# A written order for the opening of a chunked-attention and mixture kernel: 128-token loads, own PSUM banks, later units moved

## The chip, the cores and the metric

The kernel runs on one NeuronCore of a Trainium2 chip. The metric is the device time of one execution in microseconds (us). TensorE is PE here, its weight loads PEld, VectorE DVE, ScalarE ACT, GpSimd POOL and SyncE SP; SP issues nearly all DMA transfers.

## The reference

Queries, keys and values are 8 x 8 x 576 x 64 in float32. Attention goes over chunks of 64 tokens that don't see each other; its output is one row of 512 numbers for each of 4608 tokens, which then goes through a root-mean-square norm and a gated layer of width 1536.

```python
scores = scale * np.matmul(q_c, k_c.transpose(0, 1, 2, 4, 3))     # chunks of 64
scores = scores - np.max(scores, axis=-1, keepdims=True)
attn = np.exp(scores)
attn = attn / (np.sum(attn, axis=-1, keepdims=True) + 1e-09)
out = np.matmul(attn, v_c)
...
rms = np.sqrt(np.mean(x * x, axis=-1, keepdims=True) + 1e-06)
xn = x / rms * rms_g
g = xn @ w_gate
silu = g * (1.0 / (1.0 + np.exp(-g)))
val = xn @ w_val
return (silu * val @ w_out).astype(np.float32)
```

## The kernel before

**Numbers in two parts.** The large products keep float32 accuracy by splitting each number into a high part and a low part, which PE multiplies fast (hi·hi, lo·hi, hi·lo: three products for one). The activations are split when x is turned: ACT writes the high part xh with the norm's weight (`x_split`, L523), DVE the low part xl (L524). The weights arrive as float32 in `raw` tiles of 1 MB and are converted once, in 18 conversions: on ACT an absolute value and a scaling (L189, L190), on DVE a clamp, a shift and two word operations (L198, L199, L200, L203; the last is a custom instruction on 16-bit words), on ACT a cast to the high part (L214), on DVE the subtraction that leaves the low part (L220). `conv_start`, `conv_join` and `conv_end` are these three pieces; `conv_step` does one step of each for three neighbouring conversions and starts the next load.

**Tiles and units.** The tokens form nine tiles of 512. Attention goes by units of 256 tokens, two to a tile; a unit has two blocks of 128 tokens. For a block: scores on PE (`scores`, L269), maximum and subtraction on DVE (L282, L283), exponential on ACT (L286), sums and their reciprocal on DVE (L291 to L293), transposing of the weights through PE (L329) with a copy on ACT (L330), values on PE (L451), division by the sums on DVE (L482), mean square on ACT (L470), an addition on DVE (L471), a power on POOL (L473), scaling on ACT (L488), transposing of x on PE (L554), and the split.

**Tile 0.** Units 0 and 1 are the opening; the scheduler of the framework decides in which order each engine takes the opening's instructions. Then come twelve steps f of the gated layer: `gated` does the up products of 128 columns (L565), the gate on ACT (L583) and DVE (L587), and `down` the products with the output weights (L629). During these steps the weights are converted, ahead of the step that multiplies by them, and units 2 and 3 are computed for tile 1 (scores at f 0 and 5, transposes at f 2 and 7, values at f 3 and 8, scaling at f 4 and 9).

**Tiles 1 and 2, and the pairs.** From tile 1 on the order on PE, DVE, ACT, SP and POOL is that of the code. Tiles 1 and 2 have 24 half-steps each (up products in L606, gate in L619 and L621). The remaining six tiles go in pairs with seven products in place of eight (L794, L975), whose combined weights ("sides", L659 to L676, L695 to L729) are made in tiles 1 and 2. Units 4 to 9 are computed there, at the half-steps that a table `UNIT_AT` gives, a row for a unit. Their weights are turned by way of memory: `turn_away` (L367) and `turn_back` (L377, into tile eT), values in L392, x turned by DVE (L423), sent away (L428) and brought back (L435). All of these transfers stand in SP's one queue.

## Time and profile before

| | |
|---|---|
| three runs | 903.3, 905.18, 905.21 us; median 905.18 |
| the profiled execution | 903.54 us, its span 901.8 us |
| PE busy in the span | 875.2 us, 97% |
| PEld, DVE, ACT, POOL busy | 79%, 75%, 49%, 19% |
| granted PE clock, mean | 0.998 of full |

The span is the time between the first and the last recorded instruction; 1.7 us of the execution lie outside of it. A share of the whole span is a mean over the opening, tile 0, tiles 1 and 2 and the pairs, which load the engines differently.

### The profile page before, as it was taken

The numbers are of one execution on the slowest core, as the hardware profiler recorded it, in microseconds if no ns is written. First come the engines' busy times: TensorE is split into PE (matmuls) and PEld (weight loads), VectorE is DVE, ScalarE is ACT, GpSimd is POOL, SyncE is SP. The second block draws the span as 40 slices with busy tenths as digits, with TensorE's granted clock in tenths as the row PEclk, the third lists the DMA queues.
The fourth block names the chain that finished last, engine by engine and source line by source line (L and its number), as shares of the span: only waits on it lengthen the run. The fifth ranks groups of instructions, "written<-read, shape, count | busy, mean of one in ns | idle before, by whom it ended". The sixth has DMA issues, their size and how long they took to land.

```text
span 901.8 us, 17138 instructions
## 1 busy us (share of the span) xinstructions
PE 875.2 (97%) x6792; PEld 715.4 (79%) x6792; DVE 672.1 (75%) x1083; ACT 438.1 (49%) x733; POOL 171.6 (19%) x213
## 2 busy tenths in 40 slices
PE   5799999999999999999999999999999999999998
PEld 4588878877888888888877888888878888888886
DVE  6999996788686887876577988756679974345885
ACT  5997944446353663433355644334536532112452
POOL 0100005395670000112221001122210002111000
PEclk9999999999999999999999999999999999999999
DMA  9698966879879967489877884898689677445623
GB/s 358 267 376 311 312 242 218 268 240 289 252 232 312 293 240 266 162 308 350 259 271 233 302 300 164 303 291 316 238 255 330 256 297 266 152 156 191 217 72 116
DMA packets 96512, 231.82 MB, mean 257 GB/s; under 512 B 7344, under 2 KB 63664, under 8 KB 81072
## 3 DMA queue, kind: packets, MB, share of 16 engines
q1 hardware_dynamic: 95376, 230.19, 73.9%
q8 instruction: 54, 0.88, 0.4%
q10 hardware_dynamic: 1056, 0.52, 0.2%
q14 instruction: 26, 0.21, 0.1%
HBM read 171.97 MB, written 58.72 MB: 256 GB/s over the span
## 4 chain that ended last, share of the span: by engine, by line
PE 74%; DVE 8%; issue 6%; ACT 6%; DMA 4%; POOL 1%; SPq 1%; ACTq 0%; DVEq 0%; POOLq 0%
PE ps_a L794 10%; PE ps_c L794 10%; PE ps_b L794 10%; PE ps_a L975 7%; PE ps_b L975 7%; PE ps_c L975 6%; PE ps_d L794 5%; PE ps_g L606 5%; PE ps_v L606 4%; PE ps_d L975 4%; PE ps_s L269 1%; PE ps_o L392 1%; DMA wr<-wsd 1%; PE acc L629 1%; DVE ab L723 1%
## 5 line engine op out<-in xcount | busy, mean ns | idle before, releaser
L894 ACT CAST gh<-g 128x512 fp32r<-128x512 f32 x140 | 81.7, 620 | 75.5 <-PE ps_b L975 21.3
L895 DVE TENSOR_TENSOR gl<-g,gh 128x512 fp32r<-128x512 f32 x140 | 95.3, 688 | 30.3 <-ACT gh L894 29.3
L794 PE MATMUL ps_c<-xp,wr 128*128 128x512 f32 x432 | 104.7, 391 | 0.0
L794 PE MATMUL ps_b<-xp,wr 128*128 128x512 f32 x432 | 104.4, 391 | 0.0
L794 PE MATMUL ps_a<-xp,wr 128*128 128x512 f32 x432 | 103.7, 390 | 0.4 <-DMA wr<-wsd 0.4
L794 PEld LDWEIGHTS ps_a<-xp,wr 128*128 128x128 f32 x432 | 80.9, 188 | 17.6 <-issue 0.8
L794 PEld LDWEIGHTS ps_c<-xp,wr 128*128 128x128 f32 x432 | 80.7, 188 | 17.1
L794 PEld LDWEIGHTS ps_b<-xp,wr 128*128 128x128 f32 x432 | 80.6, 188 | 16.9
L859 POOL TENSOR_TENSOR g<-c,c 128x512 f32<-128x512 f32 x18 | 23.2, 1291 | 359.1 <-DVE c L855 269.0
L606 PE MATMUL ps_g<-xh,parts 128*128 128x512 f32 x192 | 65.8, 396 | 1.1 <-ACT sg L619 1.1
L606 PE MATMUL ps_v<-xh,parts 128*128 128x512 f32 x192 | 66.2, 398 | 0.0
L975 PE MATMUL ps_a<-gh,wo 128*128 128x512 f32 x176 | 55.9, 389 | 0.0
L794 PE MATMUL ps_d<-xp,wr 128*128 128x512 f32 x216 | 51.9, 389 | 0.0
L975 PE MATMUL ps_c<-gh,wo 128*128 128x512 f32 x160 | 51.1, 392 | 0.2 <-ACT gh L894 0.2
L975 PE MATMUL ps_b<-gh,wo 128*128 128x512 f32 x160 | 50.5, 389 | 0.0
L794 PEld LDWEIGHTS ps_d<-xp,wr 128*128 128x128 f32 x216 | 40.5, 188 | 8.4
L937 DVE TENSOR_TENSOR g<-g 128x512 f32<-128x512 f32 x68 | 46.6, 686 | 0.0
L835 ACT ACTIVATE c<-c 128x512 f32<-128x512 f32 x18 | 11.4, 635 | 68.1 <-DVE c L855 68.0
L606 PEld LDWEIGHTS ps_v<-xh,parts 128*128 128x128 f32 x192 | 36.3, 189 | 10.1 <-issue 2.1
L606 PEld LDWEIGHTS ps_g<-xh,parts 128*128 128x128 f32 x192 | 36.5, 190 | 9.6 <-ACT sg L619 1.6
L844 DVE TENSOR_TENSOR u<-ps_b,p 128x512 f32<-128x512 f32 x36 | 24.0, 685 | 25.2 <-PE ps_b L794 24.0
L695 POOL TENSOR_TENSOR ab<-parts 128x256 f32<-128x256 f32 x48 | 37.3, 810 | 23.5 <-DVE xl L524 23.5
(176 smaller groups left out, 1872.3 us busy)
## 6 DMA issues: line engine op xcount, KB each, us to landing
wr<-wsd SPq DMA_DIRECT2D x63, 1024.0 KB, 8.5
qk<-qk_dram SPq DMA_DIRECT2D x17, 1024.0 KB, 6.9
wo<-wol SPq DMA_DIRECT2D x16, 1024.0 KB, 8.0
raw<-w_up_dram SPq DMA_DIRECT2D x12, 1024.0 KB, 13.0
wo<-wod SPq DMA_DIRECT2D x12, 1024.0 KB, 9.4
vt<-v_dram SPq DMA_DIRECT2D x18, 512.0 KB, 5.8
wsd<-parts SPq DMA_DIRECT2D x18, 512.0 KB, 8.3
wo<-wol SPq DMA_DIRECT2D x16, 512.0 KB, 7.6
```

What stands on the lines that cost most here:

```text
L269: nc.tensor.matmul(st["s"][j][c * CH : (c + 1) * CH, pr], st["q"][rows, pr, tok : tok + CH], st["k"][rows, pr, tok : tok + CH], start=True ...
L392: nc.tensor.matmul(st["o"][(2 * c + t) * Q : (2 * c + t + 1) * Q, h * D : (h + 1) * D], eT[rows, c, t, h], vt[rows, c, h], start=True, sto ...
L606: nc.tensor.matmul(ps[k], a, b[dt], start=(dt == 0 and i == 0), stop=(dt == NDT - 1 and i == 2), skip_group_check=True,)
L695: return nc.gpsimd.tensor_tensor(out, one, two, op=op)
L794: nc.tensor.matmul(ps, w[:, a, m, cols], xp[:, b, kt], start=start and kt == 0 and i == 0, stop=stop and kt == 1 and i == 2, skip_group_ch ...
L835: nc.scalar.activation(t, t if src is None else src, AF.Silu)
L844: nc.vector.tensor_tensor(kp["u2"], b["b"], kp["p1"], op=add)
L859: nc.gpsimd.tensor_tensor(g[1][1], kp["c22"], kept[0]["c22"], op=mult)
L894: nc.scalar.copy(gh, src)
L895: nc.vector.tensor_tensor(gl, src, gh.bitcast(F32), op=ALU.subtract)
L937: nc.vector.tensor_tensor(out, one, two, op=ALU.subtract)
L975: nc.tensor.matmul(ps[m][INTO[p]], w[:, m, a], parts[c], start=p in FROM and i == 0 and j == 0, stop=p in LAST and i == NPR - 1 and j == 2 ...
```

## The change

- Queries and keys are laid out by blocks of 128 tokens, so that a block's are 4 KB in one piece for each partition. The opening loads four blocks by four transfers of 512 KB on SP, ahead of the values, the weights and the norm's weight; four more weight tiles follow the first where three did.
- The whole opening, from the loads to the last split, is put under a written order for five engines. `softmax`, `norm`, `x_transpose_unit`, `conv_start` and `conv_join` are cut into pieces for it. Maximum and subtraction alternate for the two halves of a block. The scores of each block have own PSUM banks. The transposed weights go to the tiles `gl` and `gh`. The reciprocals of two blocks are taken at once.
- The mean square uses the function of the later units (`mean_square`): addition and power both on POOL.
- Only conversion 0 is done in the opening. The ACT part of conversions 2 to 7 is tied behind the last high part of the split (`tokens_first`).
- The first up products take all of hi·xh of gate and value first, then lo·xh, then hi·xl (`up_first`).
- Unit 2 is computed at f 1, 3, 4 and 5, unit 3 at f 6, 8, 9 and 10.
- In `UNIT_AT`, units 6 and 7 load their values, take back the turned weights and multiply by the values at earlier half-steps (unit 6: 16, 16, 25 become 13, 15, 18; unit 7: 27, 27, 32 become 20, 21, 26), and what follows moves with them.

```diff
+LATER = 7
+UNITS_AT = {1: (2, 0), 3: (2, 1), 4: (2, 2), 5: (2, 3), 6: (3, 0), 8: (3, 1), 9: (3, 2), 10: (3, 3)}
...
-    (5, 10, 16, 12, 14, 16, 25, 27, 27, 28, 31),
-    (11, 15, 27, 17, 19, 27, 32, 34, 34, 35, 38),
+    (5, 10, 13, 12, 14, 15, 18, 20, 20, 21, 25),
+    (11, 15, 20, 17, 19, 21, 26, 28, 28, 29, 32),
...
+    def tokens_first(ins, n):
+        if 1 < n <= LATER:
+            info = mybir.DependencyInfo(mybir.DependencyClass.NoSync, mybir.DependencyReason.DATA)
+            tc.add_manual_dep(ins.ins, first_last[0].ins.name, info, reason="tokens are split first")
...
-    def load_first_unit():
-        qt, kt = (x[:, 2 * i : 2 * i + 2].rearrange("p s (a t) -> p (s a) t", t=UT) for i in range(2))
-        for s in range(2):
-            part = slice(s * P, (s + 1) * P)
-            nc.sync.dma_start(qt[:, :, part], qk[0][:, 0, :, part])
-            nc.scalar.dma_start(kt[:, :, part], qk[0][:, 1, :, part])
-            state[s] = {"q": qt, "k": kt}
+    def load_sub(i, t):
+        t = t.rearrange("p (w a t) -> p w a t", w=2, t=P)
+        nc.sync.dma_start(t, qk[i // 2][:, i % 2])
+        state[i] = {"q": t[:, 0], "k": t[:, 1]}
...
+    def up_first():
+        pg, pv = bank(ps_h, "ps_g"), bank(ps_h, "ps_v")
+        for i in range(3):
+            for ps, wh, wl in ((pg, wgh, wgl), (pv, wvh, wvl)):
+                a, b = ((wh, xh), (wl, xh), (wh, xl))[i]
+                for dt in range(NDT):
...
-    load_first_unit()
+    first_ordered = tc.manual_schedule(engines={*engines, mybir.EngineType.Pool})
+    first_ordered.__enter__()
+    for i in range(2):
+        load_sub(i, x[:, 2 * i : 2 * i + 2].rearrange("p s c -> p (s c)"))
...
     conv_load(0)
-    load_values(0)
-    load_unit(1)
+    nc.sync.dma_start(g_col, rms_g)
     load_values(1)
...
+    norm_square(3)
+    conv_words(0)
+    x_split_half(0, 0)
+    norm_scale(2)
+    x_split_half(0, 1)
+    conv_high(0)
+    norm_scale(3)
+    for half in range(2):
+        x_transpose_half(1, half, ps_acc)
+    conv_end(0)
+    for half in range(2):
+        x_split_half(1, half)
+    conv_start(1)
+    first_ordered.__exit__(None, None, None)
+    conv_step(EARLY - 1)
```

DVE in the later part of the opening, before, with the weight conversions among the attention's instructions (L198 and L199 clamp and shift, L200 and L203 word operations, L220 a low part of weights, L524 low parts of x):

```order
41 L199 TENSOR_SCALAR w<-w 128x1024
42 L524 SCALAR_TENSOR_TENSOR xl_125<-ps_x,g_col,xh_121 128x256
43 L471 TENSOR_SCALAR ss<-ss 128x1
44 L200 SCALAR_TENSOR_TENSOR w<-raw,w 128x1024
45 L220 TENSOR_TENSOR parts<-w,parts 128x1024
46 L524 SCALAR_TENSOR_TENSOR xl_126<-ps_x,g_col,xh_122 128x256
49 L203 ISA w<-raw,w 128x2048
51 L198 TENSOR_SCALAR w<-w 128x1024 x2
52 L199 TENSOR_SCALAR w<-w 128x1024 x2
53 L200 SCALAR_TENSOR_TENSOR w<-raw,w 128x1024
54 L524 SCALAR_TENSOR_TENSOR xl_123<-ps_x,g_col,xh_119 128x256
56 L203 ISA w<-raw,w 128x2048
```

The same place after the change (L220 and L223 are now the word operations, L249 the low part of weights, L569 the low part of x, L212 and L213 clamp and shift):

```order
33 L220 SCALAR_TENSOR_TENSOR w<-raw,w 128x1024
34 L223 ISA w<-raw,w 128x2048
35 L569 SCALAR_TENSOR_TENSOR xl_123<-ps_x,g_col,xh_119 128x256
36 L569 SCALAR_TENSOR_TENSOR xl_124<-ps_x,g_col,xh_120 128x256
39 L249 TENSOR_TENSOR parts<-w,parts 128x1024
42 L569 SCALAR_TENSOR_TENSOR xl_125<-ps_x,g_col,xh_121 128x256
43 L569 SCALAR_TENSOR_TENSOR xl_126<-ps_x,g_col,xh_122 128x256
44 L212 TENSOR_SCALAR w<-w 128x1024
45 L213 TENSOR_SCALAR w<-w 128x1024
46 L220 SCALAR_TENSOR_TENSOR w<-raw,w 128x1024
47 L212 TENSOR_SCALAR w<-w 128x1024
48 L223 ISA w<-raw,w 128x2048
```

Clamps, shifts and word operations of conversions 1 to 3 stood ahead of the last xl; they stand behind it now, and only the word operations of conversion 0 are ahead of the first.

ACT at the splits after the change, with what each instruction waits for in brackets (L568 high parts of x, L533 scaling of a block, L237 cast of a conversion's high part, L190 and L194 the ACT part of conversions):

```order
17 L568 ACTIVATE xh_119<-ps_x,g_col 128x256 [waits DMAHW6_49,PE_49]
18 L568 ACTIVATE xh_120<-ps_x,g_col 128x256 [waits DVE_49]
19 L533 ACTIVATE x<-x,ri_t 128x512 [waits Activation_49,Pool_49]
20 L568 ACTIVATE xh_121<-ps_x,g_col 128x256 [waits PE_49]
21 L568 ACTIVATE xh_122<-ps_x,g_col 128x256 [waits DVE_49]
22 L237 CAST parts<-w 128x1024
23 L533 ACTIVATE x<-x,ri_t 128x512 [waits Activation_49,Pool_49]
24 L568 ACTIVATE xh_119<-ps_x,g_col 128x256 [waits PE_49]
25 L568 ACTIVATE xh_120<-ps_x,g_col 128x256 [waits DVE_49]
28 L190 ACTIVATE w<-raw 128x1024 [waits DMAHW0_49]
29 L194 ACTIVATE raw<-raw 128x1024
```

Every second high part waits for DVE (the low part that reads the same bank), and L190 and L194 of conversions from 1 on stand behind all high parts; before, four of L189 and six of L190 stood ahead of the last one, one of each for conversion 0.

SP in tile 1, before, at unit 6 (L367 and L377 send away and bring back the turned weights of unit 6, L428 sends x of unit 5, L676 stores combined weights, L245 loads the values of unit 6):

```order
87 L367 DMA away_e12_2203<-e_1984 128x512
88 L367 DMA away_e13_2205<-e_1991 128x512
89 L428 DMA away_x5_2220<-xu_2118 128x1024
90 L676 DMA wol_130<-parts_926 512x1x256 x2
91 L245 DMA vt_2304<-v_dram 128x1024
92 L377 DMA eT_2306<-away_e12_2203 32x4x256 x2
93 L377 DMA eT_2306<-away_e13_2205 32x4x256 x2
94 L728 DMA wsd_128<-side_2270 128x512
```

And after the change (L413, L423, L474, L742 in their places; the values are loaded at row 84):

```order
84 L275 DMA vt_2170<-v_dram 128x1024
89 L413 DMA away_e12_2205<-e_1984 128x512
90 L413 DMA away_e13_2207<-e_1991 128x512
91 L474 DMA away_x5_2222<-xu_2118 128x1024
92 L423 DMA eT_2224<-away_e12_2205 32x4x256 x2
93 L423 DMA eT_2224<-away_e13_2207 32x4x256 x2
94 L742 DMA wol_130<-parts_924 512x1x256 x2
```

The four loads of eT stand one place behind unit 5's x now, with the values ahead of them and the stores behind.

## Rows read from the trace of the kernel before

**Rows 1.** The page, part 1: busy us of each engine, its share of the span, and its instructions.

```profile
PE 875.2 (97%) x6792; PEld 715.4 (79%) x6792; DVE 672.1 (75%) x1083; ACT 438.1 (49%) x733; POOL 171.6 (19%) x213
```

**Rows 2.** Busy time by stretch, the opening and tile 0: start and end (us), length, busy us of each engine with its instructions, granted PE clock as a share of full, DMA share, GB/s.

```profile
0.00:37.24 37.24, 21.18 (x294) 15.65 (x294) 27.66 (x62) 25.89 (x41) 4.44 (x11) 1.00 0.90 353
37.24:132.00 94.76, 93.19 (x651) 76.50 (x651) 92.69 (x121) 78.09 (x149) 2.75 (x2) 1.00 0.83 296
```

**Rows 3.** Timeline of PE: start (us), duration, line, operation, out<-in, count, and in brackets the idle time before it with what ended it.

```profile
4.88 1.13 PE L269 MATMUL ps_s<-x 64*64 64x64 f32 x32 [4.88 <-DMA x<-qk_dram]
6.63 1.13 PE L269 MATMUL ps_s<-x 64*64 64x64 f32 x32 [0.62 <-DMA x<-qk_dram]
...
33.10 1.11 PE L554 MATMUL ps_x<-ident,x 128*128 128x128 f32 x4 [3.53 <-ACT x L488]
34.42 0.80 PE L565 MATMUL ps_g<-xh,parts 128*128 128x512 f32 x1 [0.20 <-ACT xh L523]
...
37.24 0.65 PE L565 MATMUL ps_g<-xh,parts 128*128 128x512 f32 x1
...
123.83 0.50 PE L565 MATMUL ps_g<-xh,parts 128*128 128x512 f32 x1 [1.57 <-ACT sg L583]
...
190.37 0.39 PE L606 MATMUL ps_v<-xl,parts 128*128 128x512 f32 x1 [1.92 <-issue]
...
208.74 0.39 PE L606 MATMUL ps_v<-xh,parts 128*128 128x512 f32 x1
...
212.76 0.50 PE L606 MATMUL ps_g<-xh,parts 128*128 128x512 f32 x1 [1.14 <-ACT sg L619]
```

**Rows 4.** Transfers from 0 to 60 us, in 40 slices of 1.5 us: GB/s moved in each.

```profile
GB/s 0 122 338 326 421 388 426 423 424 405 404 410 431 431 421 415 415 399 437 431 404 401 399 90 5 0 0 5 344 268 289 399 431 363 254 362 447 431 421 379
```

**Rows 5.** Groups of DVE's instructions from 20.8 to 38.2 us: line, operation, out<-in with shapes, count | busy us, mean ns of one | idle time before.

```profile
L524 DVE SCALAR_TENSOR_TENSOR xl<-ps_x,g_col,xh 128x256 fp32r<-128x256 f32 x8 | 3.7, 480 | 0.7 <-ACT xh L523 0.7
...
L200 DVE SCALAR_TENSOR_TENSOR w<-raw,w 128x1024 int32<-128x1024 int32 x2 | 2.4, 1219 | 0.0
L203 DVE CUSTOM_DVE_ANT_0 w<-raw,w 128x2048 uint16<-128x2048 uint16 x2 | 2.4, 1218 | 0.0
L198 DVE TENSOR_SCALAR w<-w 128x1024 f32<-128x1024 f32 x3 | 2.0, 689 | 0.0
L199 DVE TENSOR_SCALAR w<-w 128x1024 int32<-128x1024 int32 x3 | 1.9, 674 | 0.0
L482 DVE TENSOR_TENSOR x<-ps_o,rs 128x256 f32<-128x256 f32 x4 | 1.6, 418 | 0.7 <-PE ps_o L451 0.7
L291 DVE TENSOR_REDUCE rs<-e 128x8 f32<-128x512 f32 x1 | 0.7, 686 | 0.0
L293 DVE RECIPROCAL rs<-rs 128x8 f32<-128x8 f32 x2 | 0.4, 196 | 0.0
L292 DVE TENSOR_SCALAR rs<-rs 128x8 f32<-128x8 f32 x2 | 0.3, 164 | 0.0
```

**Rows 6.** Timeline of ACT in the opening and at the first gate.

```profile
21.20 0.47 ACT L523 ACTIVATE xh<-ps_x,g_col 128x256 fp32r<-128x256 f32 x1
...
26.13 1.05 ACT L214 CAST parts<-w 128x1024 fp32r<-128x1024 f32 x1
...
27.47 0.72 ACT L488 ACTIVATE x<-x,ri 128x512 f32<-128x512 f32 x1
...
38.39 1.15 ACT L190 ACTIVATE raw<-raw 128x1024 int32<-128x1024 uint32 x1
39.55 1.28 ACT L583 ACT_TABLE_LOAD   x1
40.85 0.60 ACT L583 ACTIVATE sg<-ps_g 128x512 f32<-128x512 f32 x1
```

**Rows 7.** Timeline of POOL in the opening.

```profile
25.98 1.46 POOL L473 TENSOR_TENSOR ri<-ss,mhalf 128x1 f32<-128x1 f32 x1 [6.94 <-DVE ss L471]
```

**Rows 8.** Timeline of DVE: the last low parts of x, the last low part of weights in tile 0, and tile 1 at the turning of x and the softmax of unit 6.

```profile
37.22 0.88 DVE L524 SCALAR_TENSOR_TENSOR xl<-ps_x,g_col,xh 128x256 fp32r<-128x256 f32 x2 [0.71 <-ACT xh L523]
...
129.61 1.22 DVE L220 TENSOR_TENSOR parts<-w,parts 128x1024 fp32r<-128x1024 f32 x1
130.74 0.42 DVE L667 TENSOR_TENSOR w<-w 128x256 f32<-128x256 f32 x1
...
204.11 1.25 DVE L423 STREAM_TRANSPOSE xu<-xu 128x1024 f32<-128x1024 f32 x1 [0.46 <-ACT xu L417]
...
205.85 0.41 DVE L341 TENSOR_REDUCE mx<-ps_s 128x4 f32<-128x256 f32 x1
206.30 0.42 DVE L342 TENSOR_TENSOR e<-ps_s,mx 128x256 f32<-128x256 f32 x1
```

**Rows 9.** Tile eT from 200 to 260 us: duration min/median/max in ns with first and last start, and the times from issue to landing.

```profile
L392 PE MATMUL ps_o<-vt,eT x256: 213/216/240, 230.0 to 253.3; 64*32 64x64 f32 x128
...
DMA to landing us min/median/max: 4.3/4.9/5.6
```

**Rows 10.** Timeline of SP in tile 1: transfers issued.

```profile
205.38 0.32 SPq L428 DMA_DIRECT2D away_x<-xu  x1
...
208.60 2.74 SPq L377 DMA_DIRECT2D eT<-away_e  x4
```

**Rows 11.** Busy time by stretch after the gap before 190.37 (columns as in rows 2).

```profile
191.19:194.61 3.42, 3.42 (x10) 2.63 (x9) 3.28 (x9) 1.55 (x4) 3.01 (x7) 0.50 0.91 243
```

More of the change, by code (lines that the diff above doesn't have):

```diff
@@ L181, in conv_load, with conv_abs, conv_low @@
             nc.sync.dma_start(raws[n], w_up[f] if kind == "up" else w_out[f // 2])
+    def conv_abs(n):
+        words = raws[n].bitcast(I32).rearrange("p (n w) -> p n w", w=2)
+        low, high = words[:, :, 0], words[:, :, 1]
+        w = wp.tile([P, 2 * DM], F32, name="w")
+        conv[n] = low, high, w
+        tokens_first(nc.scalar.activation(w, high.bitcast(F32), AF.Abs, scale=2.0**16), n)
+    def conv_low(n):
+        low = conv[n][0]
+        tokens_first(nc.scalar.mul(low, low.bitcast(U32), 2.0**-29), n)
@@ L188, in conv_start, with conv_clamp, conv_words @@
-            conv[n] = low, high, w
-            nc.scalar.activation(w, high.bitcast(F32), AF.Abs, scale=2.0**16)
-            nc.scalar.mul(low, low.bitcast(U32), 2.0**-29)
+            conv_abs(n)
+            conv_low(n)
+    def conv_clamp(n):
+        w = conv[n][2]
+        wi = w.bitcast(I32)
+        nc.vector.tensor_scalar(w, w, HIGH_LEAST, HIGH_MOST, op0=ALU.max, op1=ALU.min)
+        nc.vector.tensor_single_scalar(wi, wi, 3, op=ALU.logical_shift_left)
+    def conv_words(n):
+        low, high, w = conv[n]
+        wi = w.bitcast(I32)
+        nc.vector.scalar_tensor_tensor(
+            wi, high, -(2**31), wi, op0=ALU.bitwise_and, op1=ALU.bitwise_or
+        )
+        nc.vector.tensor_tensor(wi, wi, low, op=ALU.add)
@@ new lines, in conv_high @@
+    def conv_high(n):
+        w = conv[n][2]
+        parts = wts.tile([P, 2, 2, DM], F32R, tag="wts", name="parts")
+        (conv_parts if pairs[n][0] == "up" else out_parts).append(parts)
+        conv[n] = w, parts
+        kind, f = pairs[n]
+        if kind == "up":
+            homes = (wgh, wgl, f), (wvh, wvl, f)
+        else:
+            homes = (woh, wol, f), (woh, wol, f + 1)
+        for i, (hi, lo, at) in enumerate(homes):
+            hi[at], lo[at] = parts[:, 0, i], parts[:, 1, i]
+        nc.scalar.copy(parts[:, 0].rearrange("p i c -> p (i c)"), w)
@@ L205, in conv_join @@
-            (conv_parts if pairs[n][0] == "up" else out_parts).append(parts)
-            conv[n] = w, parts
-            kind, f = pairs[n]
-            if kind == "up":
-                homes = (wgh, wgl, f), (wvh, wvl, f)
-            else:
-                homes = (woh, wol, f), (woh, wol, f + 1)
-            for i, (hi, lo, at) in enumerate(homes):
-                hi[at], lo[at] = parts[:, 0, i], parts[:, 1, i]
-            nc.scalar.copy(parts[:, 0].rearrange("p i c -> p (i c)"), w)
+            conv_clamp(n)
@@ L216, in conv_end @@
+            conv_words(n)
+            conv_high(n)
     def conv_end(n):
-        if 0 <= n < len(pairs):
+        if n in conv:
             w, parts = conv.pop(n)
@@ L1080, in __call__ @@
             self.n += 1
-    load_first_unit()
+    engines = mybir.EngineType.PE, mybir.EngineType.SP, mybir.EngineType.DVE, mybir.EngineType.Activation
+    first_ordered = tc.manual_schedule(engines={*engines, mybir.EngineType.Pool})
+    first_ordered.__enter__()
+    for i in range(2):
+        load_sub(i, x[:, 2 * i : 2 * i + 2].rearrange("p s c -> p (s c)"))
+    t = io.tile([P, 2, 2, NPAIR, P], F32, tag="qk", bufs=1, name="qk")
+    for s in range(2):
+        load_sub(2 + s, t[:, s].rearrange("p w a t -> p (w a t)"))
@@ L1096, in tile_chunk_attn_swiglu @@
-    softmax_sum(0)
-    att_transpose(1)
+    for i in range(2):
+        softmax_less(i)
+        softmax_exp(i)
+    copied = att_transpose(0, later=True)
+    scores(2, s2)
+    softmax_sum(0)
+    copied()
+    copied = att_transpose(1, later=True)
+    scores(3, s3)
+    softmax_sum(1)
+    softmax_turned(0)
+    copied()
+    softmax_less(2)
+    softmax_exp(2)
+    conv_abs(0)
     o = two_banks(ps_h, "ps_o")
     att_values(0, o)
-    softmax_sum(1)
+    copied = att_transpose(2, later=True)
@@ L1115, in tile_chunk_attn_swiglu @@
+    att_values(3, o)
+    norm_scale(0)
     norm(2)
-    att_values(3, o)
+    norm_square(2)
+    norm_scale(1)
+    for half in range(2):
+        x_transpose_half(0, half, ps_a)
     norm(3)
-    x_transpose_unit(1)
-    conv_start(0)
-    conv_step(EARLY)
+    norm_square(3)
[8 more added lines that the diff above has]
+    conv_end(0)
+    for half in range(2):
+        x_split_half(1, half)
@@ L1161, in tile_chunk_attn_swiglu @@
         evacuate(acc, 0, s)
-    engines = mybir.EngineType.PE, mybir.EngineType.SP, mybir.EngineType.DVE, mybir.EngineType.Activation
     ordered = tc.manual_schedule(engines=set(engines))
@@ L1311 @@
     arrays = {
[L1312 removed]
+        "qk": np.stack([heads_first(q), heads_first(k)], axis=3),
         "v": vv,
```

160 lines of the change are left out of this document (87 added, 73 removed).

## The prediction

> **What bounds the kernel now.** I read the engines' shares first: PE is busy 875.2 of 901.8 us, no other engine over three quarters [rows 1]. Then the span is cut where the matmuls become continuous. Up to 37.24 us PE has only 21.18 us of work, which is the opening that the change writes down anew; from 37.24 to 132 it is busy 93.19 of 94.76 [rows 2]. The reader should see the other column of that second row: DVE is busy 92.69 of the same 94.76. In tile 0, where the weights are converted, DVE is as full as PE, with 2.07 us to spare; ACT has 16.67.
>
> PE's timeline shows where it stands still, with the wait in brackets: the first score waits 4.88 for queries and keys, the last transposes 3.53 for the scaled x, the first product of the MoE comes at 34.42; from 37.24 the products are continuous, with gaps of 1.57, 1.92 and 1.14 before 123.83, 190.37 and 212.76 [rows 3]. So time can be won in the opening, and it stays won only if DVE, next in line, lets PE keep its lead.
>
> **The loads.** The first block's scores wait for its queries and keys until 4.88, the second's until 6.63 [rows 3]. They come in pieces of 512 bytes. In the transfer row the slices of 1.5 us from 3 to 6 us moved 338 and 326 GB/s, and those from 6 us on about 420 [rows 4]. After, pieces are 4 KB and these 512 KB come alone. At 420 GB/s they take 1.25 us; from the slice that begins at 1.5 us (122 GB/s, transfers starting in it) that gives 3.6 at the earliest. I bound the landing by 3.6 and by 4.88, and take 4.4.
>
> The row gives the 512-byte pieces a fifth less. The Trainium skill, "DMA: Bandwidth & Descriptors", section Specifications, puts the least size for line rate at 512 bytes; by that the new layout would gain nothing and the landing stay at 4.88, half a microsecond in the sum.
>
> **DVE through the opening.** After, DVE's order is a straight line from the first scores to the first splits. From 4.4 the scores take 1.13 [rows 3], so DVE starts at 5.5. Four blocks of reduce and subtract: the new order makes them dependent pairs, j by j, and such a pair stands later in the trace at 205.85 and 206.30 [rows 8]: 0.45 from start to start, and 0.34 for the second, since neighbours overlap by about 0.08 (129.61 + 1.22 ends 0.09 after 130.74). So 2 x 0.79 = 1.58 a block, 6.3 in all; the old order, two of each kind in a row, has no such pairs. The other pieces by their means, less 0.08 each: four sums at 0.60 make 2.4, two turnings at 0.08 + 0.12 0.4, eight norm halves at 0.34 2.7, the clamp and shift of conversion 0 at 0.60 1.2, its two word operations at 1.14 2.3 [rows 5]. A sum that needs the exponential just before it, and a turning that needs its sums, can't overlap; I add 0.08 for each of some ten of these, 0.8. In all 16.1: DVE reaches the first low split at 21.6 if it never waits. Between 6.01 (4.88 + 1.13) and 37.24 it idled 31.23 - 27.66 = 3.6 [rows 2, 3]; I take half of that, 1.8, and get 23.4 (21.6 to 25.2).
>
> Then ACT and DVE alternate, since the second high part of a bank waits for DVE's low part of the first: low 0.48, high 0.47, the scale of block 2 0.72, high 0.47, low 0.48, high 0.47, the cast of conversion 0 1.05, the scale of block 3 0.72, its transposes 1.11 of which half before the first bank is full, high 0.47 [rows 3, 5, 6]. That is 5.9, less the overlap of 0.08 where two stand in a row on ACT 5.7: the first MoE product at about 29.1 instead of 34.42, 5.3 earlier (bounds 27.2 to 30.9). Four further splits, alternating at about 0.95 each but the first, end at 31.9 instead of 37.22 + 0.88 = 38.10 [rows 8]: 6.2 earlier.
>
> **Moves that cost nothing by themselves.** The mean square's addition leaves DVE (0.15 a block) for POOL, where the power of one column took up to 1.46 [rows 5, 7]; an addition of one column is bounded by nothing and by that, and I take 1 between them. It lies beside DVE's norms for blocks 0 to 2; block 3's has the 2.3 of words and three splits as cover, and without that cover it costs 1. Own banks for the scores and the gl and gh homes of the transposed weights let PE run ahead of DVE; PE isn't what is waited for there. The product order of the first up needs the high parts only, for 8 products. Units 2 and 3 keep their instructions; unit 3 is scaled at f 10 in place of 9 and its x is turned at f 11, so a step of 94.76 / 12 = 7.9 us covers it; the uncovered price would be its two scalings, 1.4 [rows 2, 6].
>
> **What is owed.** Here I expect the gain to go. By 38.10 the old DVE order had finished, besides conversion 0, the clamps and shifts of conversions 1 to 3 and the word operations of 1 and 2: from 20.8 to 38.2 three clamps (L198, 0.69), three shifts (L199, 0.67) and two of each word operation (L200, L203, 1.22) [rows 5]. Less 0.08 each that is 1.8 + 1.8 + 2.3 + 2.3 = 8.1 us of DVE work that the change puts behind the last split. The last split is 6.2 earlier, so DVE is 1.9 later in tile 0 than now, less the 2.07 of idle that it can use [rows 2]: -0.2 to +1.9. The conversions are what PE multiplies by, and the last low part, from 129.61, is ready 1.2 us before tile 0's end at 132 [rows 8]; so PE can end the tile between 1.4 earlier and 1.9 later. Not all idle can be used, as DVE waits for ACT's casts, which start late too: I take +0.6. The 5.3 us won up front show up as waits for converted weights, spread over tile 0.
>
> ACT gets four more table loads in tile 0: 1.28 each [rows 6], 5.1 of its 16.67 idle; hidden, except where a cast stands behind one. The row shows the next instruction starting 0.02 after the load ended (39.55 + 1.28, then 40.85), and the one before it ended as it began: no drain is seen.
>
> The Trainium skill, "ScalarE: Activation LUTs", section What ACT_TABLE_LOAD costs, gives a switch 1.283 us for the load and 1.38 for a drain, 2.66 in all. By it the four take 10.6 us of ACT, an estimate from that page, and the sum would rise by up to 5.5.
>
> **Tile 1.** Unit 6's values move from half-step 25 to 18. Now they start at 230.0, and their transposed weights, issued from 208.60 on and 4.3 to 5.6 us in landing, are there some 14 us ahead [rows 9, 10]. After, they are issued right behind unit 5's x, which leaves at 205.38 when DVE's turn of 204.11 + 1.25 is done [rows 8, 10]; SP holds them behind that. From 205.7 the first lands at 210.0 or later, a fourth issued about 1.5 behind and landing in 4.9 at 212.1 [rows 9]. PE reaches half-step 18 at 208.74 [rows 3]. It waits 1.3 to 3.4, with the down and up products queued behind. Most of now's 1.14 before 212.76 goes into that wait, as ACT catches up: net +0.2 to +2.3. I take +0.3, near the landing's minimum, as 1 MB of stores now goes behind these pieces. The gap of 1.92 before 190.37 has no releaser in the trace; I keep it.
>
> **Sum.** 903.54 + 0.6 + 0.3 = 904.4 against the profiled run's own time. The three runs of before have a mean of 904.56, 1.02 above that run; with that 905.5, which I give as the median.
>
> **Rivals.**
> - *The lead is kept.* If the new interleaving packs DVE and ACT better than I assume, 5.3 comes off: 898.2, with the 1.02 899.3; half of it gives 901.9. For it: PE idles 16 of the first 37 us. Against: DVE's 92.69 of 94.76. Decided by whether DVE's last conversion ends before 127. Chance 0.30.
> - *Slower by the late transfer.* Place: PE at half-step 18. A wait of 3.4, less the 1.14, is +2.3; and after the 1.92 gap the clock was granted at 0.50 from 191.19 to 194.61, the lower level of 1.2 GHz [rows 11], where the 3.42 cost 1.7. Together +4.0, with 0.6 for tile 0: 909.2. It decides once the last piece lands after 211. Against: after the 1.57 before 123.83 the clock stayed [rows 2]. Chance 0.14.
> - *The opening is not shorter.* POOL at 1.46 an operation and the word operations ahead of the splits eat half the 6.2: then DVE is 8.1 - 3.1 - 2.07 = 2.9 late, 907.8. Chance 0.07.
> - *The table loads aren't hidden.* If each of the four stands in front of a cast that PE waits for, 4 x 1.28 = 5.1 come on top: 910.6. Against: 16.67 of idle on ACT, and the 0.02 above. Chance 0.05. (The rule of that page of the Trainium skill would act in this way.)
>
> **How the numbers follow.** The forecast has 0.44. A measurement of this kernel tells about 0.2%, 1.8 us, from no change, since its three runs differ by that: 903.4 to 907.0 is "same". Faster is the first rival, 0.30; slower the three others, 0.26. The forecast's own range, by the bounds of tile 0 and tile 1, is 903 to 908. To hold 8 in 10 the range takes in the greater part of the first rival and the cheaper half of the slow ones: 900.8 to 909.0.
>
> **What would show it.** First product of the MoE near 29 and last low split near 32 (right opening); DVE over 97% from there to 132, and PE idle about 5 us in tile 0, ended by ACT's cast or DVE's low part (right debt); tile 1's first product within 2 us of now's; a PE wait of 1 to 3.4 at the third values of tile 1. The prediction is wrong if PE stays continuous after 32, or if DVE has more idle time than 2 us by 132.

## The result, and the profile after

The changed kernel takes 910.32 us (median; 909.19 to 912.76) against 904.73 for the kernel before, a ratio of 1.0068 with a 95% interval of 1.0044 to 1.0092: 5.6 us slower, and above the forecast range of 900.8 to 909.0. The profiled execution is the slowest of the four, 912.76 with a span of 911.0. Two executions further on, one with the old table (1245.52 us) and one of the kernel before beside it (2656.29 us), were disturbed and are left out of times and ratios.

Engines of the kernel after, first the busy line, then the granted clock by 40 slices of the span (to be held against [rows 1]):

```profile
PE 881.1 (97%) x6792; PEld 715.0 (78%) x6792; DVE 675.4 (74%) x1075; ACT 442.6 (49%) x737; POOL 172.9 (19%) x217
...
PEclk8799999998999999999999999999999999999999
```

DVE, ACT and POOL have nearly the same work as before. PE is busy 5.9 us more with the same 6792 products: they are slower, not more. Of the 40 slices of the clock the first and the tenth have an 8 and the second a 7; all others have 9.

Busy time by stretch, as in [rows 2], with the first cut at the changed kernel's first product:

```profile
0.00:29.20 29.20, 14.97 (x283) 11.74 (x284) 18.79 (x41) 15.59 (x28) 5.76 (x15) 0.80 0.95 367
29.20:37.24 8.04, 8.04 (x31) 5.81 (x31) 5.70 (x10) 6.35 (x9) 0.00 (x0) 0.65 0.79 299
37.24:132.00 94.76, 91.13 (x624) 71.32 (x623) 91.42 (x117) 84.25 (x150) 1.69 (x1) 1.00 0.81 291
```

PE's clock was granted at 0.80 on average up to 29.2 and at 0.65 until 37.24, where the row of the kernel before has 1.00 (its products there did not run at full pace either, as the part on the half clock shows). In tile 0 DVE is a little less full than it was, 91.42 of 94.76 for 92.69, and PE idles 3.6 us where it idled 1.6.

Timeline of PE, to be held against [rows 3]:

```profile
4.92 1.13 PE L296 MATMUL ps_s<-x 64*64 64x64 f32 x32 [4.92 <-DMA x<-qk_dram]
6.63 1.13 PE L296 MATMUL ps_s<-x 64*64 64x64 f32 x32 [0.58 <-DMA x<-qk_dram]
...
16.83 0.66 PE L369 MATMUL ps_t<-ident,e 128*128 128x128 f32 x4 [1.61 <-ACT e L316]
...
29.02 1.54 PE L597 MATMUL ps_x<-ident,x 128*128 128x128 f32 x6 [2.26 <-ACT x L533]
30.27 0.80 PE L627 MATMUL ps_g<-xh,parts 128*128 128x512 f32 x1
...
41.81 0.73 PE L612 MATMUL ps_g<-xh,parts 128*128 128x512 f32 x2 [0.86 <-DVE parts L249]
...
60.11 0.96 PE L695 MATMUL acc<-parts,gh 128*128 128x512 f32 x3 [1.22 <-ACT parts L237]
...
193.15 0.40 PE L672 MATMUL ps_v<-xh,parts 128*128 128x512 f32 x1 [2.58 <-issue]
...
212.05 0.27 PE L438 MATMUL ps_o<-vt,eT 64*32 64x64 f32 x2 [1.75 <-DMA eT<-away_e]
213.65 1.65 PE L438 MATMUL ps_o<-vt,eT 64*32 64x64 f32 x100 [1.33 <-DVE ab L789]
```

The first scores start no earlier than before (4.92 and 6.63). The first product of the MoE comes at 30.27 instead of 34.42. Then PE waits for converted weights (L237 the high part, L249 the low part), which it never did before. In tile 1 it waits 1.75 and 1.33 for unit 6's turned weights: the second bracket names DVE, but the second of the four pieces lands at 211.91 and the fourth at 213.51, each 0.14 before PE goes on.

Where the time went, from the traces of the two profiled executions (us; the pairs begin with the first product into ps_a). These two are 1.2 below and 2.4 above their medians, so that they differ by more than the medians do:

| | before | after | difference |
|---|---|---|---|
| first product of the MoE | 34.42 | 30.27 | -4.15 |
| last low part of x, end | 38.10 | 33.18 | -4.92 |
| first product of tile 1 | 144.79 | 147.08 | +2.29 |
| first product of the pairs | 307.67 | 312.14 | +4.47 |
| last product | 897.86 | 906.85 | +8.99 |

Between the last two lines lies what the prediction has no word on: 4.5 us are lost in the pairs, whose code the change doesn't touch.

### The profile page after: what moved, and what is told of

It reads as the page before. It is cut to its first block, busy times and chain, and to the rows that moved or that the text cites. A ratio compares the mean times of both kernels' runs of the same rounds, so it can differ in the third digit from the quotient of the medians.

```text
span 911.0 us, 17152 instructions
## 1 busy us (share of the span) xinstructions
PE 881.1 (97%) x6792; PEld 715.0 (78%) x6792; DVE 675.4 (74%) x1075; ACT 442.6 (49%) x737; POOL 172.9 (19%) x217
## 4 chain that ended last, share of the span: by engine, by line
PE 78%; DVE 9%; ACT 5%; DMA 4%; issue 2%; SPq 1%; POOL 0%; ACTq 0%; DVEq 0%
PE ps_a L860 10%; PE ps_c L860 10%; PE ps_b L860 10%; PE ps_a L1041 7%; PE ps_b L1041 7%; PE ps_c L1041 7%; PE ps_v L672 5%; PE ps_g L672 5%; PE ps_d L860 5%; PE ps_d L1041 4%; PE ps_o L438 2%; PE acc L695 2%; PE ps_s L296 1%; DMA raw<-w_up_dram 1%; PE ps_v L612 1%
## 5 line engine op out<-in xcount | busy, mean ns | idle before, releaser
L960 ACT CAST gh<-g 128x512 fp32r<-128x512 f32 x140 | 81.4, 618 | 78.7 <-PE ps_b L1041 29.1
L925 POOL TENSOR_TENSOR g<-c,c 128x512 f32<-128x512 f32 x18 | 23.3, 1296 | 361.3 <-DVE c L921 277.8
L761 POOL TENSOR_TENSOR ab<-ab 128x256 f32<-128x256 f32 x48 | 41.9, 878 | 2.8
```

Of the source, the lines that this page charges most:

```text
L761: return nc.gpsimd.tensor_tensor(out, one, two, op=op)
L925: nc.gpsimd.tensor_tensor(g[1][1], kp["c22"], kept[0]["c22"], op=mult)
L960: nc.scalar.copy(gh, src)
```

## The experiments

**One exponential, and unit 6's table.** Four runs took the changes apart. The first moves one line of the opening, since the page above shows the last block's transposes waiting 1.61 for its exponential, and ACT at that time waiting for a weight tile:

```profile
15.14 1.12 ACT L190 ACTIVATE w<-raw 128x1024 f32<-128x1024 f32 x1 [1.60 <-DMA raw<-w_up_dram]
...
36.88 1.28 ACT L649 ACT_TABLE_LOAD   x1
38.17 0.60 ACT L649 ACTIVATE sg<-ps_g 128x512 f32<-128x512 f32 x1
```

```diff
     softmax_exp(2)
-    conv_abs(0)
     ...
     softmax_exp(3)
+    conv_abs(0)
     norm(0)
```

> The changed kernel with one move in the opening's order: the last block's exponential stands ahead of conversion 0's absolute value on ACT, so that it does not wait behind a weight tile that lands at 15.1 us. If ACT's order is what made the opening long, the exponential starts near 14.5 instead of 16.16, the PE gap of 1.61 before 16.83 closes, the first product of the MoE comes near 28.7 instead of 30.27, and the last low part of x near 31.6 instead of 33.19. If tile 0 then ends by the conversions (debt theory) and these begin as much earlier, tile 1 begins 1 to 1.6 earlier than at 147.08. If the half clock from 17.8 to 34.6 is what costs, it stays away and 2 us more come back. If neither, tile 1 begins at 147 as now.

Measured: 911.48 us, ratio 1.0085 [1.0070, 1.0100]; first product at 29.80, last low part at 32.71, tile 1 at 146.76. The gap moved behind the transposes: 2.36 before the second values, ended by DVE's division (L520). In seven other runs with the unchanged opening the first product came at 28.8 to 29.1. In four of them (the old table, no clamps, and the two with padding below) ACT waited 0.22 to 0.40 for the weight tile in place of 1.60, so it had landed earlier: 30.27 is one execution's late landing and not ACT's order. The theory falls. Of use is what stays equal: tile 1 begins 116.8 us after the first product in the changed kernel and 117.0 here.

The second and third exchange the table `UNIT_AT`, one in each kernel:

```diff
-    (5, 10, 13, 12, 14, 15, 18, 20, 20, 21, 25),
-    (11, 15, 20, 17, 19, 21, 26, 28, 28, 29, 32),
+    (5, 10, 16, 12, 14, 16, 25, 27, 27, 28, 31),
+    (11, 15, 27, 17, 19, 27, 32, 34, 34, 35, 38),
```

> The changed kernel with the UNIT_AT table of before (units 6 and 7 back at their old half-steps). If the early units cost what tile 1 lost (waits of 1.75 and 1.33 before the values of unit 6, then 6.8 us at half clock), the median falls by 2.5 to 3.5 us, to about 907, and the loss that is left is tile 0's 2.3. If tile 1's loss is only passed on from tile 0 (DVE late there), the median stays at 910.

Measured: 908.60 us over three executions, 1.0059 [1.0043, 1.0076]. Here the opening shows what it does when the weights land in time: first product 28.81, last low part 31.72; tile 1 begins at 145.56, the pairs at 308.45, 0.8 later than before. The wait for unit 6 is gone. Yet the time is that of the changed kernel less 1.7: the loss in the pairs is all there.

> The kernel before with the changed UNIT_AT table alone. If the table by itself makes PE wait for unit 6's weights, PE stands still 1.3 to 3.4 us at the third values of tile 1 and the time rises by 1 to 4 us. If the wait needs the late tile 0 of the changed kernel, there is no wait and the time is that of before within 1 us.

Measured: 906.47 us, 1.0027 [1.0011, 1.0044]. The table by itself makes the wait. Timeline of PE in this run (its profiled execution, 909.33 us, is one of the two slowest of ten):

```profile
190.74 0.40 PE L606 MATMUL ps_v<-xl,parts 128*128 128x512 f32 x1 [1.71 <-issue]
...
209.55 0.27 PE L392 MATMUL ps_o<-vt,eT 64*32 64x64 f32 x2 [1.90 <-DMA eT<-away_e]
211.15 1.96 PE L392 MATMUL ps_o<-vt,eT 64*32 64x64 f32 x120 [1.33 <-DVE ab L723]
```

1.90 and 1.33 at the third values of tile 1; the 1.71 ahead of them has no releaser, like the 1.92 in [rows 3].

The fourth takes work from DVE in tile 0:

```diff
-        nc.vector.tensor_scalar(w, w, HIGH_LEAST, HIGH_MOST, op0=ALU.max, op1=ALU.min)
+        if n < 2:
+            nc.vector.tensor_scalar(w, w, HIGH_LEAST, HIGH_MOST, op0=ALU.max, op1=ALU.min)
```

> The changed kernel with the clamp of conversions 2 to 17 left out (0.6 us of DVE each, 9.6 us in all; the weights' high parts are not held in range then). If DVE's debt sets the end of tile 0, PE's waits for parts go and tile 1 begins 2 to 3 us earlier than at 147.08. If the half clock of the opening set it, tile 1 begins where it did, within 0.5.

Measured: 912.24 us, 1.0099 [1.0073, 1.0125]; tile 1 at 147.35. PE reached the x transposes at the end of tile 0 at 137.21, 108.3 us after its first product, where the changed kernel needed 109.5: 1.2 us for 9.6 us less on DVE. Then it lost more: ACT waited 4.89 for the reciprocal root of unit 3 on POOL, which took 5.36. The scheduler had also put other work in other places, so the run doesn't settle what the debt costs.

**The pairs: 128 bytes.** In the pairs the output products are slower. Groups of the page, kernel before, then after (count, busy us, mean ns of one):

```profile
L975 PE MATMUL ps_a<-gh,wo 128*128 128x512 f32 x176 | 55.9, 389 | 0.0
...
L975 PE MATMUL ps_c<-gh,wo 128*128 128x512 f32 x160 | 51.1, 392 | 0.2 <-ACT gh L894 0.2
L975 PE MATMUL ps_b<-gh,wo 128*128 128x512 f32 x160 | 50.5, 389 | 0.0
```

```profile
L1041 PE MATMUL ps_a<-gh,wo 128*128 128x512 f32 x176 | 56.6, 393 | 0.0
L1041 PE MATMUL ps_c<-gh,wo 128*128 128x512 f32 x160 | 51.7, 395 | 1.3 <-issue 1.2
...
L1041 PE MATMUL ps_b<-gh,wo 128*128 128x512 f32 x160 | 51.3, 394 | 0.0
```

389 to 392 ns have become 393 to 395; in the last three of the four output stages (756 products with gl or gh) the next product starts 232 ns after the one before instead of 227, in the median. Same code, same order, granted clock 1.00. What differs is the place: the pool of small tiles is 128 bytes a partition smaller in the changed kernel (two groups of tiles of the norm are gone, one is larger), and so gl, part of gh and the temporary tiles, which are allocated behind it, start at 199744, 201792, ... instead of 199872, 201920, ... The weights wo stay where they were, and so does the rest of gh, which lies where xh and xl did. Divided by 256, the addresses of wo and of the other homes of operands leave 192 in both kernels; gl and that part of gh leave 192 before and 64 after. Two runs moved them, by an unused tile of 128 bytes:

```diff
     nc.gpsimd.memset(mhalf, -0.5)
+    nc.gpsimd.memset(small.tile([P, 32], F32, tag="pad", bufs=1, name="pad"), 0.0)
```

> The changed kernel with 128 unused bytes a partition put into the pool of small tiles, nothing else. They move gl, gh and the temporary tiles to addresses that leave 192 by 256, as in the kernel before (199744 and on become 199872 and on); gl still stands ahead of gh. If the place of these tiles is what makes the down products of the pairs run at a product every 232 ns in place of 227, the pitch is 226.7 again in all of them and the median falls by about 4 us, to 906. If the slower pitch is from the order of gl and gh, from the order of work or from the loads, pitch and time stay: 910.

Measured: 905.18 us, 1.0016 [1.0003, 1.0029] to the kernel before. By the two ratios to the kernel before, 0.52% or 4.7 us come back from 128 unused bytes. The group of the page:

```profile
L1042 PE MATMUL ps_a<-gh,wo 128*128 128x512 f32 x176 | 55.8, 389 | 0.0
```

> The kernel before with the same 128 unused bytes: gh, gl and the temporary tiles move from 199872 and on to 200000 and on (64 by 256). If their place sets the pitch, the down products of the pairs run at 232 and the time rises by about 4 us, to 908 to 909, with the opening and tiles 0 to 2 as before. If not, the time is that of before.

Measured: 908.39 us, 1.0049 [1.0034, 1.0064]. The same bytes make the kernel before 0.49% or 4.4 us slower, and its products like those of the changed one:

```profile
L976 PE MATMUL ps_a<-gh,wo 128*128 128x512 f32 x176 | 56.5, 393 | 0.0
```

So the place of these tiles is the cause, shown from both sides. Four more runs, of one execution each, asked for the rule; what counts in them is the pace of the products, not the time.

> The changed kernel with 64 unused bytes in place of 128: gl, gh and the temporary tiles leave 128 by 256. If the pitch of the down products goes by whether the products' two operands start alike (all of the other tiles leave 192 by 256), it is slow here too, about 232. If only the place 64 by 256 is slow, it is 226.7.

> The changed kernel with 192 unused bytes: gl, gh and the temporary tiles leave 0 by 256. If unlike places are slow, the pitch of the down products is about 232; if only 64 by 256 is, it is 226.7.

Measured: 910.24 and 910.20 us. Both are slow, by the groups of the page with 64 and then with 192 bytes:

```profile
L1042 PE MATMUL ps_a<-gh,wo 128*128 128x512 f32 x176 | 56.4, 392 | 0.0
```

```profile
L1042 PE MATMUL ps_a<-gh,wo 128*128 128x512 f32 x176 | 56.6, 394 | 0.0
```

Then everything was moved, with the unused tile ahead of all but three constants, in the kernel before and in the changed one:

```diff
+    nc.gpsimd.memset(const.tile([P, 32], F32, name="pad"), 0.0)
     mhalf = const.tile([P, 1], F32, name="mhalf")
```

> The kernel before with 128 unused bytes ahead of all tiles but three constants: all operands of the products leave 64 by 256, alike. If what matters is that the two operands of a product (gl or gh, and the weights) start alike, the pitch of the down products is 226.7 and the time that of before. If 64 by 256 is a slow place in itself, it is 232 and the time 4 us more.

> The changed kernel with the same 128 bytes ahead of all tiles: gl, gh and the temporary tiles leave 192 by 256 as in the fast kernels, the weights and the home of the other operands 64. If unlike places are slow, the pitch is 232 as in the changed kernel and the time 910; if 192 is the fast place for gl and gh whatever the weights have, it is 226.7 and 905.

Measured: 905.68 and 911.69 us beside 905.82 for the kernel before. First the kernel before with all operands at 64, then the changed one with gl and gh at 192 and the weights at 64:

```profile
L976 PE MATMUL ps_a<-gh,wo 128*128 128x512 f32 x176 | 55.9, 390 | 0.0
```

```profile
L1042 PE MATMUL ps_a<-gh,wo 128*128 128x512 f32 x176 | 56.6, 393 | 0.0
```

All alike at 64 is fast, and 192 against 64 is slow. In these kernels the output stages are fast when all tiles that they read leave the same remainder by 256, whether that is 192 or 64. It isn't a matter of one product's own two operands: in the changed kernel 320 output products read gh and wo both at 192, and their median is 230 ns all the same. Two things stay open. In the fast layouts all starts are alike by 512 too, so that no run tells 256 from 512 (by 128 they are alike in slow ones as well, 64 and 192). And why unlike starts cost some 5 ns a product is not shown: the neighbouring products' reads, or other engines' work on the moved tiles, are both possible.

**The opening's gain.** With the place repaired, the rest of the change can be read.

> The changed kernel with the padding and with the UNIT_AT table of before. If the two causes add up, it is 4 us below the run with the old table alone (909.2): 905, within 1 us of the kernel before, and tile 1 begins 0.8 to 2.3 later than before by the conversions.

Measured: 904.95 us, 1.0011 [1.0002, 1.0021]. First product 29.03, tile 1 at 145.63, 0.8 later than in the profiled execution of before, as the debt theory has it; three other traces of before's opening and tile 0 have 145.23, 145.38 and 145.70, so that this is no more than their spread. With the new table (the run with padding alone) tile 1 begins at 145.51 and the time is 905.18, so the table costs little in the median.

> The changed opening alone: padding, the UNIT_AT table of before, units 2 and 3 at their old steps, and the last exponential ahead of conversion 0's absolute value on ACT. By the debt theory tile 1 begins 0 to 1.5 later than before although the first product of the MoE is 5 us earlier, and the time is 904 to 906. If the new steps of units 2 and 3 are what tile 0 lost, tile 1 begins 1 to 3 earlier than before and the time is 902 to 903.

Measured: 911.38 us, 1.0090 [1.0065, 1.0115]. Neither: tile 1 begins at 151.02. With units 2 and 3 at their old steps PE waits 2.53 for unit 2's exponential at 59.90, and near the end of the tile ACT waits for unit 3's root. POOL and then ACT in this run:

```profile
126.39 7.42 POOL L556 TENSOR_TENSOR ri_u<-ss_u,mhalf 128x2 f32<-128x2 f32 x1 [41.43 <-DVE ss_u L554]
```

```profile
133.84 1.34 ACT L560 ACTIVATE x<-x,ri_u 128x512 f32<-128x512 f32 x2 [6.95 <-POOL ri_u L556]
```

The run also has the other place of the exponential. That begins the first product some 0.7 later (29.72), but by itself leaves the way from there to tile 1 at 117.0 us (the first run), and here it takes 121.3. The new steps of the units are no loss; this opening does worse without them.

Two ways to win the debt back were tried. One does conversion 1 in the idle gaps of the opening:

```diff
     conv_words(0)
+    conv_abs(1)
     x_split_half(0, 0)
     norm_scale(2)
+    conv_low(1)
+    conv_clamp(1)
     x_split_half(0, 1)
     conv_high(0)
     norm_scale(3)
+    conv_words(1)
     ...
+    conv_high(1)
```

> The run with padding and the old UNIT_AT, with conversion 1 done in the opening's idle gaps of ACT and DVE (its 2.3 us on ACT and 3.5 us on DVE between the splits) instead of behind the last split. By the debt theory 3.5 of the 8.1 us owed by DVE are paid from idle time: the last split is up to 2.5 later, but tile 1 begins 1 to 2.5 earlier than at 145.6, at 143 to 144.6, below the 144.8 of before, and the time is 902.5 to 904. If the conversions don't set the end of tile 0, the later first product is passed on and the time is 906 to 907.

Measured: 906.51 us, 1.0030 [1.0019, 1.0041]. The last low part came at 35.03, 3.1 later, and tile 1 at 147.65, 2.0 later. By the debt theory alone it should have come 0.4 earlier. Up to 90 us PE had no wait of 0.2 or more for parts left, but ACT stood 4.83 behind unit 2's root, which took 5.62 on POOL, and behind that PE waited 0.85, 1.65 and 0.37 for parts (95.60 to 106.80), 2.9 in all as against 3.1 without the move:

```profile
86.11 5.62 POOL L556 TENSOR_TENSOR ri_u<-ss_u,mhalf 128x2 f32<-128x2 f32 x1 [60.86 <-DVE ss_u L554]
```

How much of the 2.4 us this explains can't be told from one run; that DVE's debt alone sets the tile's end is not borne out by it.

The other keeps PE busy in the opening's gaps, to keep its clock. A first form of it computed scores again and so held the tile that unit 2's load needs (SP could issue it at 28.25 only, instead of 12.81):

> The run with padding and the old UNIT_AT, with PE kept busy in the opening's gaps: before the second values, and before each block's x transposes, the last block's scores are computed again into their own, no longer needed banks (six times 32 small products). If the half clock from about 18 to 34 us is what eats the opening's gain, the clock stays at full, the first products take 0.4 us a pair less and tile 1 begins about 2 us earlier than at 145.6, and the time is 903. If the conversions set the end of tile 0, tile 1 begins at 145.6 as without it, at full clock too, with longer waits for converted weights, and the time stays at 905.

Measured: 909.94 us, 1.0074 [1.0047, 1.0100], tile 1 at 147.22. The late load may be what spoils it; the run doesn't separate the two. The second form uses the identity:

```diff
+    def warm(n):
+        for _ in range(n):
+            for i in range(4):
+                nc.tensor.transpose(s3[i // 2][:, i % 2, :P], ident, ident)
```

> As the run with PE kept busy, but the fill is six times four transposes of the identity matrix, which hold no input tile (the scores did: unit 2's queries could be loaded at 28.25 only, in place of 12.81). Base is the run with padding and the old UNIT_AT (first product 29.0, tile 1 at 145.6, 904.95). If the half clock eats the opening's gain, tile 1 begins near 143.6 and the time is 903. If the conversions set the end of tile 0, tile 1 begins at 145.6, within 0.7, whatever the clock, and the time is 905.

Measured: 907.16 us, 1.0038 [1.0020, 1.0055]. Stretches 17 to 36 of this run, and of the run with padding and old table (the third column from the right is the granted clock):

```profile
17.00:25.00 8.00, 4.38 (x87) 3.81 (x88) 6.69 (x14) 5.78 (x14) 4.73 (x7) 1.00 1.01 418
25.00:30.00 5.00, 3.36 (x19) 2.49 (x16) 2.79 (x5) 3.12 (x6) 0.00 (x0) 0.64 1.01 415
30.00:36.00 6.00, 6.00 (x25) 4.43 (x25) 4.83 (x8) 5.40 (x7) 0.00 (x0) 0.73 0.84 332
```

```profile
17.00:25.00 8.00, 3.69 (x73) 2.87 (x74) 6.84 (x14) 5.83 (x14) 4.82 (x7) 0.71 1.02 420
25.00:30.00 5.00, 2.75 (x10) 1.76 (x10) 2.68 (x4) 3.12 (x7) 0.00 (x0) 0.50 1.00 412
30.00:36.00 6.00, 6.00 (x23) 4.33 (x23) 4.81 (x8) 5.40 (x8) 0.00 (x0) 0.67 0.85 338
```

The clock stayed full to 25 and was granted at 0.73 instead of 0.67 in the first products. Tile 1 begins at 145.44, 116.6 after the first product, as without the fill. (The profiled execution is the fastest of ten; the median is 2 us above that without the fill, and why is not known.) So the half clock of 17 to 25 is not what the opening's gain went into. For the first products themselves the run changes too little to say. The trace of the changed kernel suggests that a faster PE would win nothing there: the first wait for converted weights, 0.86 before 41.81, stands right behind them, and that low part would not be ready earlier.

No run was faster than the kernel before, clear of noise.

## Why the prediction was wrong, point by point

**What it left out: the place of the tiles.** The sum lists instructions, waits and transfers and takes each product's duration as given. That the change alters the sizes of the small tiles stands in its diff, and with it the address of everything allocated behind. This step failed: unchanged products were put down at unchanged durations, a term of nothing, and in the pairs they start every 232 ns instead of 227. The term measures 0.52% or 4.7 us in the changed kernel, 0.48% with the old table (1.0059 to 1.0011), and 0.49% in the kernel before. The other terms together were forecast at +0.9; with the place repaired they measure 0.16%, 1.4 us [0.3 to 2.6]: for them the sum holds, though partly by terms that cancel, as follows. (The down products of tile 0 read gl and gh too, and 144 of them have a median of 232 for 227: 0.7 us, of which some 0.3 is seen at tile 1, which begins 116.7 to 117.0 us after the first product without the repair and 116.5 to 116.6 with it.)

**The loads: wrong by half a microsecond.** The first block was to land at 4.4; it landed at 4.92, and between 4.67 and 5.07 in the twelve other runs with this layout. GB/s in slices of 1.5 us after, as in [rows 4]:

```profile
GB/s 0 128 325 360 289 393 434 432 411 407 431 421 421 426 426 399 421 426 410 399 378 315 374 254 82 0 16 169 421 437 371 180 382 186 404 410 339 257 436 433
```

325, 360 and 289 where 338, 326 and 421 were: pieces of 4 KB are no faster than pieces of 512 bytes. The fifth that [rows 4] seemed to give was the start of the transfers. The rule of the Trainium skill that the prediction set against it ("DMA: Bandwidth & Descriptors", Specifications) agrees with this trace.

**DVE through the opening: right in size.** Timeline of DVE after:

```profile
6.08 0.42 DVE L309 TENSOR_REDUCE mx<-ps_s 128x4 f32<-128x256 f32 x1 [6.08 <-PE ps_s L296]
6.54 0.42 DVE L310 TENSOR_TENSOR e<-ps_s,mx 128x256 f32<-128x256 f32 x1
...
24.42 0.48 DVE L569 SCALAR_TENSOR_TENSOR xl<-ps_x,g_col,xh 128x256 fp32r<-128x256 f32 x1
25.44 0.48 DVE L569 SCALAR_TENSOR_TENSOR xl<-ps_x,g_col,xh 128x256 fp32r<-128x256 f32 x1 [0.54 <-ACT xh L568]
...
32.70 0.49 DVE L569 SCALAR_TENSOR_TENSOR xl<-ps_x,g_col,xh 128x256 fp32r<-128x256 f32 x1 [0.55 <-ACT xh L568]
```

The pairs of reduce and subtract stand 0.46 apart, as taken. The first low split came at 24.42 for 23.4, and the alternation at about 1.0 each as reckoned. With the weights in time the first low split came at 23.0 to 23.3, the first product came at 28.8 to 29.1 (forecast 29.1) and the last low part at 31.7 to 32.0 (31.9). The profiled execution is 1.3 later, for ACT waited 1.60 for its weights at 15.14.

**POOL's additions and ACT's table loads: right.** An addition took 0.22, in one case 1.03. The table load before the first gate took 1.28 and the next instruction began 0.01 behind it; no drain is seen here either, against the rule of "ScalarE: Activation LUTs", What ACT_TABLE_LOAD costs, in the Trainium skill.

**Tile 0: +0.6 not refuted, the reason half right.** Tile 1 began at 145.51 and 145.63 in the two runs with the place repaired, and at 144.79 to 145.70 in four traces of before's opening and tile 0. So +0.6 fits, but can't be told from nothing. The prediction's own sign against it did come: more than 2 us of idle time on DVE by 132. From 32 to 132 DVE is busy 95.51 of 100 us in the changed kernel and 96.20 and 96.05 in the two repaired runs, where over 97% was to be seen. PE idles about 4 us there (forecast 5), 3.1 to 3.3 of it for converted parts.

That the conversions hold PE back is right all the same. Taking the products in the program's order, one finds for each of the 18 low parts of weights the first product that reads it. In the changed kernel and in the two repaired runs 10 of the 18 end less than 0.5 us ahead of that product (the closest by 0.05). In the kernel before none is closer than 1.5. The prediction had one of these margins wrong: it let tile 0 end at 132, where its row was cut. Tile 1 begins at 144.79, and the low part that is ready at 130.83 is first read at 138.67, with 7.8 us to spare and not 1.2.

But tile 1 begins 116.5 to 117.0 us after the first product in all runs with the new opening and the new steps (117.5 with the late load, 118.4 without clamps), also where 3.5 us of the debt were paid ahead. The tile acts as a fixed chain of conversions, gates and unit work that begins with the splits, 6 us longer than the 110.4 to 110.9 of before, and not as DVE's sum alone. Which link sets its length is not shown.

**Tile 1: the wait right, its net cost too small.** PE waited 1.75 + 1.33 = 3.1 (forecast 1.3 to 3.4). The fourth piece landed at 213.51, where 212.1 was reckoned at the latest. After the wait the clock was granted at 0.50; stretches of the changed kernel:

```profile
212.00:214.00 2.00, 0.62 (x31) 0.52 (x35) 1.37 (x2) 1.98 (x4) 1.84 (x3) 0.58 1.08 352
214.00:216.00 2.00, 2.00 (x121) 1.83 (x104) 0.71 (x1) 1.99 (x5) 1.92 (x3) 0.50 1.07 378
216.00:219.00 3.00, 3.00 (x8) 2.32 (x8) 2.58 (x6) 0.55 (x2) 1.57 (x3) 0.50 0.98 306
```

In the kernel before, this came after the 1.92 gap instead [rows 11]. From tile 1's first product to the pairs' it is 162.9 to 164.2 us in all runs with the old table, 163.6 to 165.1 with the new one, and 167.6 in the kernel before with it: about +1, in that one (2.9 us above its median) +4, for +0.3 taken. The rival "slower by the late transfer" had the mechanism, and the half clock, right; its 909.2 came near the result by luck, for a cause that gives a part of it only.

**The half clock of the opening: not thought of, and not new.** From 17.8 to 34.6 us the row of the changed kernel grants the lower level, 1.2 GHz, after a stretch in which PE was busy 5.0 of 5.0 us (10 to 15) and then 0.39 of 2.0. The row of the kernel before has 1.00 up to 37.24 [rows 2], but its products did not run at that pace. PE before, at its first products and where the pace changes:

```profile
35.01 0.63 PE L565 MATMUL ps_v<-xh,parts 128*128 128x512 f32 x1
35.44 0.63 PE L565 MATMUL ps_g<-xl,parts 128*128 128x512 f32 x1
...
37.73 0.39 PE L565 MATMUL ps_v<-xh,parts 128*128 128x512 f32 x1
37.95 0.40 PE L565 MATMUL ps_g<-xl,parts 128*128 128x512 f32 x1
```

And PE after, at a granted 0.50:

```profile
32.32 0.63 PE L627 MATMUL ps_g<-xh,parts 128*128 128x512 f32 x1
32.74 0.63 PE L627 MATMUL ps_v<-xh,parts 128*128 128x512 f32 x1
```

The first start 0.43 apart, like the last two, and from 37.73 on 0.22 apart. Groups of four transposes take 1.06 us or more throughout the opening of before; in the changed kernel one takes 0.66 at 16.83. So the opening of before ran at half pace too, and its 1.00 can't be read as the level there. From the first product to full pace it is 3.3 us before (34.42 to 37.73) and 4.5 after (30.27 to 34.74). At twice the time a product that costs some 0.6 us more, an estimate from these rows; the rest of the 6 us by which tile 0 is longer has other causes.

## What to carry to other kernels

A change that adds or removes even tiny tiles moves all that is allocated behind them: print the addresses of both kernels' matmul operands, and keep the starts of all that one stage reads alike. When unchanged products have another mean duration at the same clock, look at where their operands lie before looking at the schedule. Hold a granted clock of 1.00 against the pace of the products before building on it. A stage won by moving work out of the opening is won only if the next stage has an engine free to do it.

## What the runs showed of the hardware

- Output products of 32-bit words in 128 partitions and 512 columns: 227 ns from start to start where all tiles that the stage reads are alike by 256 (192 or 64), a median of 230 to 233 in the last three stages where gl and part of gh leave 64, 128 or 0 beside 192, or 192 beside 64. Products of such a stage whose own operands are alike are slow too.
- The granted clock read 1.00 in a stretch in which products started 0.43 us apart, twice the 0.22 of later.
- A power of 128x2 numbers on POOL took from 0.80 to 7.42 us. In the changed kernel:

```profile
90.15 1.69 POOL L555 TENSOR_TENSOR ri_u<-ss_u,mhalf 128x2 f32<-128x2 f32 x1 [64.27 <-DVE ss_u L553]
136.20 0.80 POOL L555 TENSOR_TENSOR ri_u<-ss_u,mhalf 128x2 f32<-128x2 f32 x1 [44.35 <-DVE ss_u L553]
```

The three long ones (5.36, 5.62 and 7.42) fall where DVE has instruction on instruction for tiles; DVE was busy 6.87 of the 7.42 us, its instructions at their usual 0.69 and 1.22. The Trainium skill, "SBUF — State Buffer", Terms, calls the ports that DVE and GpSimd share an exclusive lock whose loser waits. The traces agree in part, with POOL as the loser: two of the long ones end 0.55 us after DVE's last instruction. The third ends with DVE still at work, and DVE had no gap during the short ones above either, so what makes a power long stays open. ACT, which waits for that root in order, holds up all that is behind it.
